# Weights in long contiguous runs, queries and MLP as rows, a TensorE loop of two tiles, and the output in four column strips

## The chip, the cores and the metric

The kernel runs on one core of one Trainium2 chip. The metric is device time in microseconds (us) of that core, over several executions; lower is better. The time of a run is about 1.8 us longer than the span of its trace (1298.81 against 1297.0 for the profiled run of the kernel before); windows and instructions are on the scale of the span.

Some words: a *run* of a load is a stretch of bytes that lies together in memory (elsewhere a run is one execution of a kernel). A load is *issued* when its queue sends it off and *landed* when its data may be used. PSUM is the memory that TensorE writes; copying from there is called evacuation. A line of a TensorE listing gives start and duration in us, the engine, the line of the kernel, output<-inputs, shapes and the number of instructions; in brackets stands how long the engine had waited just before, and for whom.

## The reference, cut to what matters

```python
x  = A_x                                   # 8 sequences, 1 token, D = 640, bf16
xn = layernorm(x)
# attention with a cache: 32 heads, 4096 keys, head size 128
q      = xn @ wq                           # 640 x 4096
scores = q . k_cache * 128**-0.5           # k_cache, v_cache: 8 x 32 x 4096 x 128
o      = softmax(scores) . v_cache
a      = o @ wo                            # 4096 x 640
# channel MLP on the same xn, F = 1728
y = layernorm(xn)
m = gelu(y @ w1 + b1) @ w2 + b2            # 640 x 1728, 1728 x 640
return x + a + m
```

The two caches are 537 MB; wq and wo are 5.2 MB each, w1 and w2 2.2 MB each. All of it is read once, 552 MB in all, so the kernel is a long stream of DMA with work hung beside it.

## The kernel before

One tile t is four heads of one sequence: 4.19 MB of K and 4.19 MB of V, each 128 partitions of 32 KB. There are 64 tiles, and two buffers each for K and V. A quarter of the scores is made on TensorE (transposes of K on TensorE, then products), three quarters on VectorE. Two tiles form a group with one softmax. V is multiplied on TensorE ("PV").

The program is a list of operations. Each has a position; each engine executes its own operations in order of position, and so does the SP queue, which issues nearly all DMAs. What an operation reads (R) and writes (W) sets its semaphores. So an issue that waits in the SP queue holds up every later issue.

```python
add(eng, pos, fn, R=[...], W=[...])        # operation on engine eng, in order of pos
ld(pos, dst, src, W, sem, R=())            # the same for a DMA issued on SP

# weights of the queries in two loads; first four heads first
ld(-99.0, wqa_sb, A_wq[:, 0:QP * P].rearrange("(c k) n -> k c n", k=P), ["wqA"], "wqa")
ld(-93.0, wqb_sb, A_wq[:, QP * P:H * P].rearrange("(c k) n -> k c n", k=P), ["wqB"], "wqb")
# K of tile t at t - 1.5 (tiles 0 and 1: -100 and -94), V of tile t at t + 0.6;
# V0 and V1 lie where the weights lay: they wait for "wqBfree", "wqAfree", "ovfree"
ld(-95.2, w1_sb, B_w1.rearrange("(c k) f -> k c f", k=P), ["ovw1"], "w1")
ld(-95.1, w2_sb[:, 0:FC - 1, :], B_w2[0:(FC - 1) * P, :].rearrange("(c k) n -> k c n", k=P), ["ovw2a"], "w2a")
ld(-95.0, w2_sb[0:FLAST, FC - 1, :], B_w2[(FC - 1) * P:F, :], ["ovw2b"], "w2b")
for hg in range(NG):                       # 8 loads of wo, one for four heads
    ld(hg * B + 2.55, wo_sb[:, :, :], ..., ["wo"], "wo")
# ... (cut: layernorm, scores, softmax, values)
# end: base = x + b2 + MLP + attention of all but the last four tiles, put into PSUM by a product
# with the identity; the last projection is added on top
def pe_last(e):
    for a in range(HT):
        for k in range(2):
            r = e.matmul(TRF[0:B, k, 0:D // 2], oTn_sb[:, a, :],
                         wo_sb[:, a, k * D // 2:(k + 1) * D // 2], start=False, ...)
```

With "(c k) n -> k c n" a partition gets rows k, k+128, k+256 and so on: each row is a run of its own (1 KB for wqa, 7 KB for wqb, 3.4 KB for w1, 1,280 bytes for w2).

## Time and profile before

| quantity | value | view |
|---|---|---|
| time | 1297.73 us (1297.53 to 1297.98, 3 runs) | times |
| bytes moved | 552.04 MB | page, DMA packets |
| steady rate | 8.39 MB in 19.42 us, 432 GB/s | chain of waits, two V landings |
| VectorE, TensorE, ScalarE busy | 86%, 51%, 38% | page |
| end of the DMA stream, end of the span | about 1288.4, 1297.0 | windows of 4 us, span |

The first view is the kernel's page: the span in 40 slices of 32.4 us, with the share of the DMA engines' time (in tenths) and the rate of each slice, and the chain of waits by engine.

```profile
DMA  9999999999999999999999999999999999999997
GB/s 383 399 425 433 431 429 434 426 434 432 428 435 425 436 434 428 432 425 436 434 431 431 425 435 435 431 429 431 429 435 431 429 431 429 436 430 426 433 430 302
...
DMA 86%; PE 9%; DVE 2%; SPq 2%; issue 1%; ACT 0%; DVEq 0%
```

The DMA engines are busy everywhere. The rate is 425 to 436 GB/s from the third slice to the last but one. Only the first two slices and the last are lower, so only there can a change that moves the same bytes gain anything. What is lost in the beginning is seen in windows of 4 us. The columns are busy time of each engine, the granted TensorE clock, the DMA share and GB/s.

```profile
12.00:16.00 4.00, 0.28 (x11) 0.31 (x12) 0.00 (x0) 0.00 (x0) 0.00 (x0) 1.00 0.90 293
32.00:36.00 4.00, 0.00 (x0) 0.00 (x0) 3.96 (x2) 0.00 (x0) 0.00 (x0) 0.50 0.87 367
56.00:60.00 4.00, 3.59 (x57) 3.05 (x55) 0.00 (x0) 2.52 (x4) 0.00 (x0) 0.50 0.80 262
```

The SP queue in the beginning (start, duration, what was issued):

```profile
2.21 17.41 SPq L370 DMA_DIRECT2D w_sb<-in_B_w_dram  x2
...
30.97 0.34 SPq L370 DMA_DIRECT2D KV_sb<-in_A_k_cache_dram  x1
56.29 0.34 SPq L370 DMA_DIRECT2D KV_sb<-in_A_v_cache_dram  x1
```

The two issues of w2 (1,728 runs of 1,280 bytes) hold the queue for 17.4 us. V0 is issued at 56.29 only, when all queries are made and the place of wq is free; K2 alone was in the queue then. That is the dip at 56 to 60. The last 17 us on TensorE:

```profile
1280.06 2.30 PE L745 MATMUL TR_ps<-base_sb,ident_f 8*8 8x320 f32 x4 [0.97 <-DVE base_sb L739]
...
1286.70 1.03 PE L595 MATMUL C_ps<-rs_sb,mask_f 128*128 128x2 f32 x8
1287.66 1.49 PE L619 MATMUL PV_ps<-KV_sb,P_sb 128*16 128x512 bf16 x24
...
1290.99 0.65 PE L629 MATMUL PV_ps<-KV_sb,P_sb 128*4 128x128 bf16 x32 [0.88 <-DMA KV_sb<-in_A_v_cache_dram]
...
1292.51 2.15 PE L669 MATMUL TR_ps<-wo_sb,oTn_sb 128*8 128x320 bf16 x8 [0.26 <-DVE oTn_sb L661]
```

The window in which the stream ends, with the clock (the third number from the right):

```profile
1288.00:1292.00 4.00, 2.06 (x60) 0.84 (x48) 0.00 (x0) 0.86 (x2) 0.00 (x0) 1.00 0.10 41
```

The clock is at its full rate here: rowsum (L595) takes 1.03 us. The 41 GB/s are 0.4 us of a stream at 432, so the stream ends near 1288.4. The base product (L745) ends at 1282.36. Of tile 62's and 63's values, the last 32 PV matmuls wait 0.88 us for the last piece of V. The last projection takes 2.15 us.

### The profile page before, as it was taken

The numbers are of one execution on the slowest core, as the hardware profiler recorded it, in microseconds if no ns is written. First come the engines' busy times: TensorE is split into PE (matmuls) and PEld (weight loads), VectorE is DVE, ScalarE is ACT, GpSimd is POOL, SyncE is SP. The second block draws the span as 40 slices with busy tenths as digits, with TensorE's granted clock in tenths as the row PEclk, the third lists the DMA queues.
The fourth block names the chain that finished last, engine by engine and source line by source line (L and its number), as shares of the span: only waits on it lengthen the run. The fifth ranks groups of instructions, "written<-read, shape, count | busy, mean of one in ns | idle before, by whom it ended". The sixth has DMA issues, their size and how long they took to land.

```text
span 1297.0 us, 19542 instructions
## 1 busy us (share of the span) xinstructions
PE 657.6 (51%) x7884; PEld 428.4 (33%) x7884; DVE 1119.4 (86%) x574; ACT 493.1 (38%) x1202; POOL 0.2 (0%) x4
## 2 busy tenths in 40 slices
PE   4354554555454455444555445544545544545555
PEld 3233333333233243232333233332332332333332
DVE  7698898898898898888988888988988988988884
ACT  2244344334344244343344343343442443432442
POOL 0000000000000000000000000000000000000000
PEclk9555565555555555555555655556655565555556
DMA  9999999999999999999999999999999999999997
GB/s 383 399 425 433 431 429 434 426 434 432 428 435 425 436 434 428 432 425 436 434 431 431 425 435 435 431 429 431 429 435 431 429 431 429 436 430 426 433 430 302
DMA packets 26738, 552.04 MB, mean 426 GB/s; under 512 B 2313, under 2 KB 8801, under 8 KB 10082
## 3 DMA queue, kind: packets, MB, share of 16 engines
q1 hardware_dynamic: 26688, 551.80, 99.4%
q8 instruction: 10, 0.16, 0.1%
q10 hardware_dynamic: 34, 0.02, 0.0%
q14 instruction: 6, 0.05, 0.0%
HBM read 551.80 MB, written 0.01 MB: 425 GB/s over the span
## 4 chain that ended last, share of the span: by engine, by line
DMA 86%; PE 9%; DVE 2%; SPq 2%; issue 1%; ACT 0%; DVEq 0%
DMA KV_sb<-in_A_v_cache_dram 84%; PE PV_ps L619 8%; DMA KV_sb<-in_A_wq_dram 2%; SPq L370 2%; DVE Y_sb L544 1%; DVE Y_sb L548 0%; PE C_ps L457 0%; PE TR_ps L512 0%; ACT KT_sb L515 0%; PE TR_ps L669 0%; ACT qT_sb L462 0%; ACT S_sb L532 0%; PE PV_ps L629 0%; PE S_ps L522 0%; DVE out_sb L749 0%
## 5 line engine op out<-in xcount | busy, mean ns | idle before, releaser
L544 DVE TENSOR_TENSOR Y_sb<-KV_sb,qbc_sb 128x6144 bf16<-128x6144 bf16 x128 | 429.1, 3352 | 93.9 <-DMA KV_sb<-in_A_k_cache_dram 93.9
L551 DVE TENSOR_REDUCE S_sb<-Y_sb 128x48 f32<-128x3072 bf16 x128 | 429.1, 3353 | 4.4
L515 ACT ACTIVATE KT_sb<-TR_ps 128x1024 bf16<-128x1024 bf16 x256 | 254.8, 1021 | 249.2 <-PE TR_ps L512 247.6
L512 PE MATMUL TR_ps<-ident_bf,KV_sb 128*128 128x128 bf16 x2048 | 249.6, 309 | 102.7 <-DMA KV_sb<-in_A_k_cache_dram 84.2
L619 PE MATMUL PV_ps<-KV_sb,P_sb 128*16 128x512 bf16 x2040 | 224.6, 619 | 130.4 <-DMA KV_sb<-in_A_v_cache_dram 130.4
L512 PEld LDWEIGHTS TR_ps<-ident_bf,KV_sb 128*128 128x128 bf16 x2048 | 201.2, 142 | 115.5 <-DMA KV_sb<-in_A_k_cache_dram 89.2
L548 DVE TENSOR_TENSOR Y_sb<-Y_sb 128x3072 bf16<-128x3072 bf16 x128 | 224.9, 1757 | 4.4
L522 PE MATMUL S_ps<-qk_sb,KT_sb 128*128 128x4 bf16 x2048 | 97.9, 170 | 147.4 <-ACT KT_sb L515 145.8
L638 ACT ACTIVATE E_sb<-PV_ps 128x512 bf16<-128x512 f32 (+1 forms) x65 | 38.5, 592 | 319.8 <-PE PV_ps L619 317.9
L522 PEld LDWEIGHTS S_ps<-qk_sb,KT_sb 128*128 128x128 bf16 x2048 | 86.1, 109 | 178.2 <-ACT KT_sb L515 178.2
L619 PEld LDWEIGHTS PV_ps<-KV_sb,P_sb 128*16 128x16 bf16 x2040 | 63.1, 124 | 242.9 <-DMA KV_sb<-in_A_v_cache_dram 136.0
L583 ACT ACTIVATE P_sb<-S_sb,NB_sb 32x128 bf16<-32x128 f32 x256 | 101.9, 398 | 3.8
L644 PE MATMUL C_ps<-sel_bf,E_sb 128*128 128x4 bf16 x256 | 16.9, 172 | 102.6 <-DVE rinv_sb L600 79.3
L565 PE MATMUL CH_ps<-ident_f,M_sb 128*2 128x128 f32 (+1 forms) x33 | 12.2, 370 | 103.7 <-DVE M_sb L563 103.7
L577 ACT ACTIVATE NB_sb<-CH_ps 128x2 f32<-128x2 f32 (+1 forms) x33 | 5.7, 172 | 152.0 <-PE CH_ps L573 152.0
L532 ACT ACTIVATE S_sb<-S_ps 32x32 f32<-32x32 f32 x256 | 48.2, 188 | 31.5 <-PE S_ps L522 29.2
L644 PEld LDWEIGHTS C_ps<-sel_bf,E_sb 128*128 128x128 bf16 x256 | 11.4, 104 | 134.1 <-DVE rinv_sb L600 79.7
L595 PEld LDWEIGHTS C_ps<-rs_sb,mask_f 128*128 128x128 f32 x256 | 42.7, 252 | 24.1 <-issue 24.1
L583 ACT ACTIVATION_READ_ACCUMULATOR P_sb<-S_sb,NB_sb 32x1 f32 x256 | 47.0, 184 | 0.0
L595 PE MATMUL C_ps<-rs_sb,mask_f 128*128 128x2 f32 x256 | 45.4, 299 | 0.0
L565 PEld LDWEIGHTS CH_ps<-ident_f,M_sb 128*2 128x2 f32 (+1 forms) x33 | 2.6, 80 | 106.6 <-DVE M_sb L563 106.6
L661 DVE TENSOR_TENSOR oTn_sb<-C_ps,rinv_sb 128x8 bf16<-128x8 f32 x32 | 4.7, 147 | 26.8 <-issue 22.5
(82 smaller groups left out, 158.6 us busy)
## 6 DMA issues: line engine op xcount, KB each, us to landing
KV_sb<-in_A_k_cache_dram SPq DMA_DIRECT2D x64, 4096.0 KB, 26.8
KV_sb<-in_A_v_cache_dram SPq DMA_DIRECT2D x63, 4096.0 KB, 35.2
wo_sb<-in_A_wo_dram SPq DMA_DIRECT2D x8, 640.0 KB, 28.0
KV_sb<-in_A_wq_dram SPq DMA_DIRECT2D x1, 4480.0 KB, 28.5
KV_sb<-in_B_w_dram SPq DMA_DIRECT2D x1, 2160.0 KB, 19.2
w_sb<-in_B_w_dram SPq DMA_DIRECT2D x1, 2080.0 KB, 24.3
KV_sb<-in_A_v_cache_dram SPq DMA_DIRECT2D x1, 2048.0 KB, 12.7
KV_sb<-in_A_v_cache_dram SPq DMA_DIRECT2D x2, 1024.0 KB, 15.0
```

The lines of the kernel that those rows point to most:

```text
L512: r = e.transpose(TR_ps[:, it.box[0], jj * P:(jj + 1) * P], kv[:, n * BK + jj, :], ident_bf[:, :])
L515: add("act", t - 0.59 + 0.12 * n, lambda e: e.activation(KT_sb[:, m % NS, :, :].rearrange("p a b -> p (a b)"), TR_ps[:, it.box[0], :], ACT ...
L522: r = e.matmul(S_ps[:, c:c + HT], KT_sb[:, m % NS, jj, :], qk_sb[:, :, b % HB], start=True, stop=True)
L532: r = e.activation(S_sb[s, g % SR, i, 0:JP], S_ps[s, 0:JP * HT].rearrange("p (j a) -> p j a", a=HT)[:, :, a], ACT.Copy)
L544: return e.tensor_tensor(y, kv[:, j0:j1, :], qbc_sb[:, g % 2, i, :][:, None, :].to_broadcast([P, nj, P]), ALU.mult)
L548: lambda e, y=y, y2=y2: e.tensor_tensor(y2, y[:, :, 0:P // 2], y[:, :, P // 2:P], ALU.add),
L551: lambda e, y2=y2, j0=j0, j1=j1: e.tensor_reduce(S_sb[:, g % SR, i, j0:j1], y2, AX.X, ALU.add),
L583: r = e.activation(P_sb[s, g % PR, i, :, a, :], S_sb[s, g % SR, i, :].rearrange("p (m c) -> p m c", c=4), ACT.Exp, bias=NB_sb[s, g % 2, i: ...
L595: r = e.matmul(RS_ps[:, a * GT:(a + 1) * GT], mask_f[:, a, :], rs_sb[:, g % PR, :], start=True, stop=True)
L619: r = e.matmul(PV_ps[32 * ct:32 * ct + HT * 4, t % 2, :], P_sb[:, g % PR, i, m, :, :].rearrange("p a c -> p (a c)"), vv[:, 4 * m:4 * m + 4 ...
L638: add("act", pos, lambda e: e.activation(E_sb[:, k, 0:n], PV_ps[:, k, 0:n], ACT.Copy), R=[("PV", k)], W=[("E", k)], X=[("PVb", k)])
L644: r = e.matmul(OT_i, E_sb[:, t % 2, c * P:(c + 1) * P], sel_bf[:, c:HT * 4:4], start=(c == 0), stop=(c == 3 and not last))
```

## The change

Its intent: load the weights in runs of 17 to 40 KB, so that the stream starts at full rate and the SP queue is not held; make queries and the MLP's hidden layer as rows (8 partitions, many columns, few weight loads), so that wq is done sooner and V0 can be issued sooner; make the TensorE loop two tiles long, with a projection after each pair; split the last projection into four column strips that TensorE can work on side by side. Two more edits are cut from the diff below: the probabilities of the softmax have one buffer instead of two, and the evacuation of every second tile's values waits for wo. The diff cut to its core:

```diff
-    FC = (F + P - 1) // P
+    FP, FB = 96, 4                        # 1728 = 96 x 18
+    FC, FW = F // FP, F // FB
-        w2_sb = sb("w2_sb", [P, FC, D], BF)
+        w2_sb = sb("w2_sb", [FP, FC, D], BF)
-        ld(-99.0, wqa_sb, ...); ld(-93.0, wqb_sb, ...)
+        ld(-100.0, wq_sb, A_wq.rearrange("(k c) n -> k c n", c=DC), ["wq"], "wq")
-            pos = (-100.0, -94.0)[t] if t < NK else t - 1.5         # K
+            pos = (-99.0, -94.0)[t] if t < NK else t - 1.5
-            pos = t + 0.6                                            # V
-            R = (["wqBfree"], ["wqBfree", "wqAfree", "ovfree"])[t] if t < NV else []
+            pos = (0.45, 0.55)[t] if t < NV else t + 0.6
+            R = (["wqfree"], ["wqfree", "w1free", "hfree"])[t] if t < NV else []
-        ld(-95.1, w2_sb[:, 0:FC - 1, :], ...); ld(-95.0, w2_sb[0:FLAST, FC - 1, :], ...)
+        ld(-95.1, w2_sb[:, :, :], B_w2.rearrange("(k c) n -> k c n", c=FC), ["w2"], "w2")
-            ld(hg * B + 2.55, wo_sb[:, :, :], ...
+            ld(hg * B + 3.35, wo_sb[:, :, :], ...
... (queries: 8 blocks of 5 matmuls 8 x 512 instead of 160 of 128 x 8; then 32 transposes)
-            elif (g + 1) * GT % HB == 0: ... add("pe", np_ + 0.57, pe_o, ...)
+        for g in range(-1, NGRP - 2):      # a projection for each pair of tiles; oTn zeroed in between
+            add("pe", g * GT + 5.33, pe_o, R=["wo", "oTn"], W=["ACC"], ...)
... (MLP as rows: hidden layer 4 x 432 columns, 18 transposes, second product into the PV banks)
+        add("dve", 0.2, lambda e: e.tensor_tensor(xb2_sb..., PV_ps[0:B, :, 0:D // 2], xb2_sb..., ALU.add),
+            R=["mlp", "xb2"], W=["xb2"], ...)
-                        for k in range(2): r = e.matmul(TRF[0:B, k, 0:D // 2], ...)
+                        for k in range(4): r = e.matmul(TRF[32 * k:32 * k + B, 0, 0:D // 4], ...)
-        add("sp", END + 3, lambda e: e.dma_start(out2[:, :], out_sb[:, :]), ...)
+        for k in range(4): add("sp" if k < 2 else "act", END + 3, ... out2[:, k * D // 4:(k + 1) * D // 4] ...)
-            sch.emit_rolled("pe", e, sems, 2.013, HB)
+            sch.emit_rolled("pe", e, sems, 2.27, GT)
```

## The prediction

> **What bounds the kernel.** The DMA engines. The 40-slice strip shows DMA share 9 in every slice but the last, and 425 to 436 GB/s from slice 3 to 39; the page gives 552.04 MB. The chain of waits is 83.8% "V cache landing". In the steady part a K and a V tile (8.39 MB) take 19.42 us (landings at 169.24 and 208.10 are two tiles apart): 432 GB/s. The Trainium skill ("DMA: Bandwidth & Descriptors", Where 436 GB/s comes from) puts the port ceiling at 435 GB/s; this trace agrees within 1%. VectorE is busy 86%, TensorE 51%; each K load is issued about 17 us before the queue would run dry. The change moves the same bytes, so only stretches where the queue runs below 432 GB/s, and the tail after the last landing, can give time.
>
> **Where time is lost now.** Windows of 4 us: 0-4 at 216 GB/s (first bytes, 2.0 us lost, stays), 12-16 at 293 (1.3 us; wq heads 0-3 come in 1 KB runs), 20-24 at 392 and 32-36 at 367 (0.9 together; w2 comes in 1,280-byte runs), 56-60 at 262 (1.6 us). The last is a gap: V0 may be issued only at 56.29, after wq landed at 48.8 and seven blocks of queries ran, while only K2 was queued. Against 431 GB/s, slices 1 to 3 (383, 399, 425) lack 32.4 x (48+32+6)/431 = 6.5 us, so some 4.5 can come back. Tail: last V piece 1290.95, end 1297.0; in it the projection L669 is 8 matmuls of 320 columns, 2.17 us, and the evacuations 0.48.
>
> **What the change does.**
> 1. wq whole, first in the queue, one 40 KB run per partition; w1 17 KB, w2 23 KB. The two w2 issues that held the SP queue 8.4 and 9.0 us shrink under 1 us.
> 2. Estimates from these rates: wq lands near 15 us, K0 25, w1 30, w2 35, K1 45. Queries are 40 matmuls of 512 columns, at most 0.43 us each (L619 at half clock: four side by side take 0.43), so done at 24 to 32; then V0 is issued, with over 10 us still queued. The gap at 56-60 goes. K2 is issued about 38 to 46, V1 45, K3 56 to 63: the queue stays fed.
> 3. MLP as rows: off the path.
> 4. Loop of two tiles, a projection after every pair (about 0.7 us more each), one buffer for probabilities: TensorE has the slack; steady period stays 19.42.
> 5. Tail: 16 matmuls of 160 columns in four strips. If strips overlap as in L619, 2.17 becomes about 0.6; one evacuation of 160 columns about 0.3 instead of 0.48; four output DMAs, two issues per queue, add 0.4. Net 1.4 us.
>
> Risk: w2 on 96 partitions may load the memory ports unevenly, up to 1.7 us back (estimate: a third of its 5.1 us).
>
> **Prediction.** 1297.7 - 4.3 - 1.4 = 1292.0 us (0.4% faster), range 1289.5 to 1295.0. Faster by over 2%: 0.01; within 2%: 0.985; slower: 0.005.
>
> **What would show it.** Slices 1 and 2 above 410 and 425 GB/s; no 4 us window below 380 between 4 and 100 us; SP weight issues under 1 us; V landings still two tiles per 38.85 us; last landing near 1286.5; last projection near 0.6 us; end 4.6 us after the last landing.
>
> **What would make it wrong.** The queue drains because V0 or K2 comes late; a new wait in the steady loop (projection before the wo load, single probability buffer) exceeding 17 us of slack; strips that do not overlap; small output writes that complete later.

## The result, and the profile after

The changed kernel takes 1303.14 us (1301.45 to 1304.34, 4 runs); the kernel before took 1297.86 beside it (1297.53 to 1301.29, 4 runs). The ratio is 1.0034, with a 95% interval of 1.0012 to 1.0055. A ratio here is the mean time of one kernel's runs over that of the other's of the same rounds, so it is not quite the ratio of the medians. With more rounds (e11 below) the ratio is 1.0018 (1.0004 to 1.0033). So the change costs 0.2 to 0.3%, where a gain of 0.4% was predicted.

The page of the changed kernel, the same lines:

```profile
DMA  9998999999999999999999999999999999999996
GB/s 385 378 434 379 435 434 428 429 434 429 430 434 434 425 433 435 433 424 435 432 431 428 434 429 429 434 435 424 434 435 432 431 430 432 431 429 431 432 427 292
...
DMA 57%; DVE 29%; issue 8%; PE 4%; SPq 0%; ACT 0%; DVEq 0%
```

The second and the fourth slice have fallen to 378 and 379 GB/s. The chain has moved to K and vector work, but this says little: the chain only follows one path, and the DMA share shows that the stream still fills the steady part. Two K landings of the chain (164.04 and 202.89 with the wait after them) are 38.85 us apart as before, so the steady period is unchanged.

The windows that are new:

```profile
28.00:32.00 4.00, 2.29 (x57) 1.88 (x56) 0.85 (x1) 2.39 (x6) 0.00 (x0) 1.00 1.13 334
32.00:36.00 4.00, 2.91 (x48) 2.57 (x48) 3.96 (x2) 3.53 (x5) 0.00 (x0) 0.56 1.09 242
36.00:40.00 4.00, 4.00 (x18) 1.12 (x15) 3.96 (x3) 1.53 (x2) 0.00 (x0) 0.58 1.00 243
108.00:112.00 4.00, 3.01 (x45) 2.43 (x45) 2.47 (x5) 2.42 (x10) 0.00 (x0) 0.50 0.16 47
```

There are two losses. From 28 to 40 us the DMA engines are fully busy (share 1.09, 1.09, 1.00) and yet move only 334, 242 and 243 GB/s. Against 432 that is (98 + 190 + 189) x 4 / 432 = 4.4 us. By the order of the queue w2 is being loaded then. From 108 to 112 the share is 0.16: the queue is empty for (432 - 47) x 4 / 432 = 3.6 us. The SP queue shows who let it run empty:

```profile
2.14 0.86 SPq L372 DMA_DIRECT2D w_sb<-in_B_w_dram  x1
...
28.07 0.33 SPq L372 DMA_DIRECT2D KV_sb<-in_A_v_cache_dram  x1
...
67.61 18.69 SPq L372 DMA_DIRECT2D KV_sb<-in_A_k_cache_dram  x2
...
110.25 0.39 SPq L372 DMA_DIRECT2D wo_sb<-in_A_wo_dram  x1
110.82 0.36 SPq L372 DMA_DIRECT2D KV_sb<-in_A_k_cache_dram  x1
```

w2 is issued in 0.86 us, as was hoped, and V0 at 28.07. But the first load of wo goes out at 110.25 only, and K5 (110.82) stands behind it. And VectorE has a new wait: the addition of the MLP's result waits 6.9 us for the second product.

```profile
DVE xb_sb L740 <- PE PV_ps L736: 6.9, 1, 6.9
```

The last 17 us on TensorE:

```profile
1286.66 0.72 PE L767 MATMUL TR_ps<-xb_sb,ident_f 8*8 8x160 f32 x8 [0.97 <-DVE xb_sb L761]
...
1291.73 1.84 PE L600 MATMUL C_ps<-rs_sb,mask_f 128*128 128x2 f32 x8
1293.51 2.74 PE L624 MATMUL PV_ps<-KV_sb,P_sb 128*16 128x512 bf16 x24
...
1297.15 1.05 PE L634 MATMUL PV_ps<-KV_sb,P_sb 128*4 128x128 bf16 x32
...
1299.09 0.70 PE L673 MATMUL TR_ps<-wo_sb,oTn_sb 128*8 128x160 bf16 x16 [0.26 <-DVE oTn_sb L665]
```

The strips work: the last projection takes 0.70 us, the base product 0.72. But nothing in these lines waits for DMA any more. From 1286.66 to the last 32 PV matmuls TensorE pauses only for ScalarE's evacuations (twice, 0.7 us), at half clock. Rowsum takes 1.84 us where it took 1.03 before, and the next 24 PV matmuls 2.74 where they took 1.49. The window in which the stream ends (near 1292.4):

```profile
1292.00:1296.00 4.00, 4.00 (x32) 2.19 (x31) 0.21 (x1) 0.00 (x0) 0.00 (x0) 0.50 0.11 45
```

So the two profiled runs differ in the clock at their ends too. e11 below profiles the changed kernel with the high clock.

### The profile page after: what moved, and what is told of

Same layout as the page of the kernel before. It is cut to its first block, busy times and chain, and to the rows that moved or that the text cites. A ratio compares the mean times of both kernels' runs of the same rounds, so it can differ in the third digit from the quotient of the medians.

```text
span 1302.6 us, 20062 instructions
## 1 busy us (share of the span) xinstructions
PE 680.7 (52%) x8046; PEld 440.0 (34%) x8046; DVE 1123.5 (86%) x592; ACT 499.5 (38%) x1237; POOL 0.2 (0%) x4
## 4 chain that ended last, share of the span: by engine, by line
DMA 57%; DVE 29%; issue 8%; PE 4%; SPq 0%; ACT 0%; DVEq 0%
DMA KV_sb<-in_A_k_cache_dram 56%; DVE Y_sb L549 18%; DVE Y_sb L553 6%; DVE S_sb L556 4%; DMA KV_sb<-in_A_wq_dram 1%; PE TR_ps L457 1%; PE PV_ps L736 1%; PE PV_ps L624 0%; PE TR_ps L712 0%; PE ACC_ps L684 0%; SPq L372 0%; DVE M_sb L568 0%; PE CH_ps L570 0%; PE TR_ps L725 0%; DVE M_sb L572 0%
```

## The experiments

Eleven runs were made: nine new kernels (e1 to e9), e7 once more (e10) and the changed kernel once more (e11). All gave correct results. "Before" in each call was 1297 to 1303 us, with medians of 1300.0, 1300.0 and 1299.5. Single runs of every kernel scatter by 2 to 5 us. One cause of that comes out in e4 and e7, and it limits what medians of a few runs can say. Windows and issue times are sharper.

### e1: w2 on 128 partitions

```diff
-        ld(-95.1, w2_sb[:, :, :], B_w2.rearrange("(k c) n -> k c n", c=FC), ["w2"], "w2")
+        ld(-95.1, w2_sb[:, 0:C2, :], B_w2[0:FM, :].rearrange("(k c) n -> k c n", c=C2), ["w2"], "w2")  # 13 rows each
+        ld(-95.0, w2_sb[0:R2, C2, :], B_w2[FM:F, :], ["w2b"], "w2b")                                   # 64 rows left
   (and the transposes and the second product in 13 chunks of 128 and one of 64)
```

> The changed kernel with w2 on 128 partitions again: 13 rows of 1,280 bytes in one run per partition, and 64 rows left over. Theory A (96 partitions make w2 slow, about 4.4 us of queue time lost between 28 and 40 us): no window of 4 us between 20 and 48 us below 390 GB/s. Theory B (long runs beside compute are slow): still below 300. Since the next issue behind w2 that stalls the queue, the wo load at 110 us, hangs on vector and TensorE work and not on w2, theory A further expects the gap before wo to grow from 3.6 to 5-6 us and the time to fall by only about 2 us (the second product has 28 matmuls instead of 36), to 1301. If the two losses were independent, it would fall by 4.4, to 1298.7.

Measured: 1297.89 us (1297.11 to 1299.26, 4 runs), ratio to before 0.9982 (0.9964 to 1.0000). The windows:

```profile
28.00:32.00 4.00, 3.29 (x51) 2.92 (x51) 2.79 (x1) 2.96 (x7) 0.00 (x0) 0.63 0.99 426
32.00:36.00 4.00, 3.24 (x34) 1.82 (x33) 3.93 (x3) 3.56 (x4) 0.00 (x0) 0.94 1.03 396
36.00:40.00 4.00, 3.39 (x18) 1.06 (x17) 4.00 (x2) 1.58 (x4) 0.00 (x0) 1.00 1.07 456
104.00:108.00 4.00, 2.64 (x45) 2.35 (x44) 2.89 (x4) 3.17 (x14) 0.00 (x0) 0.50 0.28 81
```

The loss from 28 to 40 us is all but gone, with runs of 16.6 KB, so theory A stands against B. The gap before wo stays (81 GB/s, and 328 in the window before it: 4.2 us together). That it would eat up most of the gain was wrong: with w2 quicker, K1 and the tiles after it land sooner, wo went out at 105.47 instead of 110.25, and the two losses added up as if independent.

### e2: the MLP addition later

```diff
-        add("dve", 0.2, lambda e: e.tensor_tensor(xb2_sb..., PV_ps..., ...
+        add("dve", 1.14, lambda e: e.tensor_tensor(xb2_sb..., PV_ps..., ...
-        add("pe", 0.3, pe_zero, ...
+        add("pe", 1.95, pe_zero, ...
```

> The changed kernel with the addition of the MLP result moved behind the vector work of tile 1, and the zeroing of PV behind it. Theory: this addition waits 6.9 us for the second MLP product with K1 landed behind it, which delays K3 and everything after by 7 us, so that the queue runs dry at 108 us. Then DVE starts tile 1 near 48.5 instead of 55.8, K3 is issued near 61, wo near 103, no window near 108 below 380 GB/s, time 3 to 4 us lower, about 1299.5. Rival (the gap comes only from the place of wo in the queue behind the projection): gap stays about 3.6 us, time unchanged.

Measured: 1301.64 us (1301.0 to 1303.48, 4 runs), ratio to before 1.0011 (0.9993 to 1.0030). The theory fell: K3 was issued at 63.32 instead of 67.61, but wo still at 109.77, and the gap stayed (67 GB/s from 108 to 112, 3.4 us). The 6.9 us that VectorE waits for the MLP are not what empties the queue. They end in an earlier wait for K2 instead.

### e3: wo behind K and V

```diff
-            ld(hg * B + 3.35, wo_sb[:, :, :],
+            ld(hg * B + 3.65, wo_sb[:, :, :],
```

> The changed kernel with each wo load moved behind the next K and V load in the SP queue. Theory: the first wo load waits for TensorE's first projection at 110.2 and holds K5, which could be issued at 102.7 when vector work on K3 is done; so the gap of 3.6 us before 111 goes and the time falls by 3 to 4 us, to 1299.5. Rival (vector work too late for any order): gap stays. No effect on steady windows in either.

Measured: 1299.35 us (1297.88 to 1301.58, 4 runs), ratio to before 0.9995 (0.9972 to 1.0018). The SP queue:

```profile
102.77 0.33 SPq L372 DMA_DIRECT2D KV_sb<-in_A_k_cache_dram  x1
...
110.13 0.39 SPq L372 DMA_DIRECT2D wo_sb<-in_A_wo_dram  x1
```

wo is issued at the same time as in the changed kernel (110.13 against 110.25), but K5 goes out at 102.77, and the window from 108 to 112 moves 426 GB/s. The gap was made by the place of the wo load in the queue. Its wait is for TensorE's projection L684, which stands behind the softmax of tiles 2 and 3 in the order of TensorE. By the code this first projection (`g = -1`) works on zeros: wo and oTn have only been set to zero by then. So the first load of wo waits for a product that adds nothing; leaving that product out was not tried.

### e4 and e7: all three edits, and two of them

e4 has the edits of e1, e2 and e3; e7 those of e1 and e3.

> All three edits together. Theory: w2 loss (4.4) and gap (3.6) both gone, so 8 us less than the changed kernel, 1295, and 2.5 us less than the kernel before. Windows between 4 and 120 us all above 380 GB/s. If there is a third loss I have not seen, it stays above 1296.5.

> w2 on 128 partitions and wo behind K and V, without the later MLP addition. Theory (the order of wo alone makes the gap; the vector wait for the MLP is made up while K2 is awaited): the same as with all three, 1293.3, no window below 380 between 8 and 120 us. Rival (the MLP wait costs by itself): 1 us or more above that.

Measured: e4 1293.34 us (1293.12 to 1296.12, 4 runs), ratio to before 0.9949 (0.9931 to 0.9967); e7 1295.55 (1293.49 to 1296.22, 4 runs), ratio 0.9969 (0.9951 to 0.9987). In both, all windows from 16 to 120 us are above 390 GB/s (that from 12 to 16 is at 383 in e4 and 375 in e7, a little under the 380 that e7's expectation set), and the stream ends alike (57 and 51 GB/s in the window from 1284 to 1288, so some 0.5 us after 1284). The intervals of the two ratios overlap. The edit of e2 brings nothing that these runs resolve.

The lowest time of each is within 0.4 us of the other's, and both have runs near 1296. The profiled runs show why. They ended with different clocks: e4 (span 1294.3) with the low one, e7 (span 1291.7) with the high one. TensorE in e4, then in e7:

```profile
1279.10 3.59 PE L627 MATMUL PV_ps<-KV_sb,P_sb 128*16 128x512 bf16 x32
...
1283.52 1.84 PE L603 MATMUL C_ps<-rs_sb,mask_f 128*128 128x2 f32 x8
1285.29 2.74 PE L627 MATMUL PV_ps<-KV_sb,P_sb 128*16 128x512 bf16 x24
...
1288.93 1.05 PE L637 MATMUL PV_ps<-KV_sb,P_sb 128*4 128x128 bf16 x32
...
1290.86 0.70 PE L676 MATMUL TR_ps<-wo_sb,oTn_sb 128*8 128x160 bf16 x16 [0.26 <-DVE oTn_sb L668]
```

```profile
1283.61 1.03 PE L603 MATMUL C_ps<-rs_sb,mask_f 128*128 128x2 f32 x8
1284.57 1.47 PE L627 MATMUL PV_ps<-KV_sb,P_sb 128*16 128x512 bf16 x24
...
1286.93 0.65 PE L637 MATMUL PV_ps<-KV_sb,P_sb 128*4 128x128 bf16 x32
...
1288.45 0.45 PE L676 MATMUL TR_ps<-wo_sb,oTn_sb 128*8 128x160 bf16 x16 [0.26 <-DVE oTn_sb L668]
```

The rowsum starts at 1283.52 and 1283.61. From there on the same instructions take 1.84 against 1.03, 2.74 against 1.47, 1.05 against 0.65 and 0.70 against 0.45 us. The granted clock from 1284 to 1288 is 0.50 in e4 and 1.00 in e7. The difference of the spans, 2.6 us, is this clock and nothing else that the traces show. The Trainium skill ("TensorE: Matmul & The Clock Gate", Part 1) describes a gate with half and full clock, set by recent activity in a free-running window of about 3.4 us, so that the moment of the switch varies from run to run. These traces agree as to the two levels and the variation; that the phase of that window decides which case a run gets is not shown here.

### e5 and e6: is it the 96 partitions?

e5 is the changed kernel with w2 on 96 partitions still, but one row of 1,280 bytes per run. e6 is the kernel before with nothing but w2 on 96 partitions, in runs of 23 KB.

```diff
 e5
-        ... B_w2.rearrange("(k c) n -> k c n", c=FC) ...      h_sb[:, j:F:FC]
+        ... B_w2.rearrange("(c k) n -> k c n", k=FP) ...      h_sb[:, j * FP:(j + 1) * FP]
 e6 (kernel before)
-        ld(-95.1, w2_sb[:, 0:FC - 1, :], ...); ld(-95.0, w2_sb[0:FLAST, FC - 1, :], ...)
+        ld(-95.1, w2_sb[:, :, :], B_w2.rearrange("(k c) n -> k c n", c=FC), ["ovw2a"], "w2a")   # FP = 96, FC = 18
-        ... w1_sb[:, kc, c * P:c * P + rows] ...
+        ... w1_sb[:, kc, c:F:FC] ...          (also b1; base_sb and out_sb share other buffers for space)
```

> The changed kernel with w2 on 96 partitions still, but in runs of 1,280 bytes (one row each) instead of 23 KB. Theory A1 (the 96 partitions are what is slow): windows between 28 and 40 us again near 240 GB/s, time 1302 to 1304. Rival A2 (runs of 23 KB at this pitch are slow, the partition count is not): these windows above 360 GB/s as with 1,280-byte runs in the kernel before, time about 1299.

> The kernel before with w2 alone changed: one run of 23 KB on each of 96 partitions, MLP in columns as it was (with strided weights), two small buffers shared. Theory A1: w2's stretch, some 15 to 30 us in, has windows near 240 GB/s, and the kernel is 3 to 4 us slower than the kernel before, about 1301 where that is 1297.7. Rival (w2 is only slow behind the wq of the changed kernel or beside its rows of MLP): no such window, time as before or 0.9 us better.

Measured: e5 1303.81 us (1301.8 to 1305.0, 4 runs), ratio to before 1.0026 (1.0005 to 1.0046); e6 1303.73 (1301.73 to 1306.39, 4 runs), ratio 1.0037 (1.0016 to 1.0057). The windows of e5, then of e6:

```profile
28.00:32.00 4.00, 3.02 (x45) 2.62 (x44) 2.48 (x1) 3.01 (x6) 0.00 (x0) 0.67 0.98 288
32.00:36.00 4.00, 3.24 (x41) 1.98 (x40) 3.93 (x3) 3.43 (x4) 0.00 (x0) 0.91 1.11 210
```

```profile
20.00:24.00 4.00, 3.22 (x45) 2.61 (x43) 3.95 (x2) 3.53 (x4) 0.00 (x0) 1.00 1.07 251
24.00:28.00 4.00, 3.77 (x26) 3.69 (x26) 3.98 (x2) 1.46 (x2) 0.00 (x0) 1.00 1.07 236
```

Short runs on 96 partitions are as slow as long ones, and in the other kernel, behind other loads and beside other work, 96 partitions are slow again. So the 96 partitions (always 0 to 95; no others were tried) are the cause, and neither the run length nor what is loaded or computed beside them. The rate is about half of 432. The Trainium skill ("SBUF — State Buffer", Door 1: The DMA port swizzle) says that partitions 0 to 63 reach only eight of sixteen memory ports and 64 to 127 the other eight, so that 64 partitions load at half the rate. It has no row for 96. Two estimates from its table and its 27.2 GB/s per port: if all ports worked to the end, the busiest, with eight of the 96 partitions, would need 6.8 us. If each of sixteen engines took six neighbouring partitions in order, which is an assumption, engines would often share a port, and the load would take 8.5 us, where 432 GB/s give 5.1 us. The windows of the changed kernel show 5.1 + 4.4 = 9.5 us. The second estimate is nearer, but no view here shows ports or which engine takes which partition, so the mechanism is argued and not shown.

### e8: what the strips are worth

All three edits of e4, with the last projection, the base product and the output as in the kernel before.

> All three edits, but the last projection in two halves of 320 columns and one output DMA, as before. My prediction's step 5 says the strips are worth 1.4 us in all: then 1294.7. From the traces (projection 2.17 to 0.70, evacuation 0.48 to 0.32, output 1.74 to 2.40) I now expect 0.9 to 1.0: 1294.3. If the base product in strips (2.3 to 0.7 us, on TensorE ahead of the last PV) counts too, 2.5: 1295.8.

Measured: 1297.14 us (1295.37 to 1299.05, 4 runs), ratio to before 0.9975 (0.9953 to 0.9998). Its profiled run has the low clock at the end, as that of e4:

```profile
1278.44 2.30 PE L773 MATMUL TR_ps<-xb_sb,ident_f 8*8 8x320 f32 x4 [0.97 <-DVE xb_sb L767]
...
1285.09 1.84 PE L603 MATMUL C_ps<-rs_sb,mask_f 128*128 128x2 f32 x8
...
1292.44 2.30 PE L676 MATMUL TR_ps<-wo_sb,oTn_sb 128*8 128x320 bf16 x8 [0.26 <-DVE oTn_sb L668]
```

The spans are 1297.1 and 1294.3. The strips save 2.8 us at the low clock: the base product 1.58 (2.30 to 0.72), the last projection 1.60 (2.30 to 0.70), the evacuation 0.16 (0.48 to 0.32), less a longer output. From the issue of the output to the end of the span e8 has 1297.1 - 1295.32 = 1.8 and e4 1294.3 - 1291.97 = 2.3 us. Of the lowest runs of each, e8 is 2.25 us above e4. So at the low clock the strips were worth about twice the 1.4 us of the prediction, which had left out the base product.

### e9, e10 and e11: the end freed from TensorE, and repetitions

e9 is e7 with the projection of tiles 58 and 59 and the base's way to rows moved from behind tile 63's softmax to before tile 62's scores. e10 is e7 again, e11 the changed kernel again.

```diff
-            add("pe", g * GT + 5.33, pe_o, ...
+            add("pe", g * GT + 5.33 if g < NGRP - 3 else 61.39, pe_o, ...
-        add("dve", fp, ... resT_sb ...); add("pe", fp + .02, pe_fin, ...); add("dve", fp + .04, dve_base, ...)
+        add("dve", 61.392, ... resT_sb ...); add("pe", 61.394, pe_fin, ...); add("dve", 61.396, dve_base, ...)
```

> As e7 (w2 on 128 partitions, wo behind K and V), and the last projection of tiles 58 and 59 and the residual's way to rows taken out of the last 4 us before PV of tile 62, to before the scores of tile 62. Theory: in all traces so far PV of tile 62 starts only when the base product ends, 22.3 us after K63's vector work starts, though its V has landed and its probabilities are ready; TensorE then has work without a gap to the end, so its granted clock decides the end (rowsum 1.03 or 1.84 us, 24 PV matmuls 1.47 or 2.74). With PV62 some 3 us earlier the last piece of V is what the end waits for: 1 us faster than e7 where the clock was high (span 1291.7), 3 us where it was low (1294.3), runs closer together, median about 1292.5. Rival (the end hangs on the last landing already): no change.

> e7 again, beside e9 on the same chip, for the difference of the two and for the spread: 1293.3 when TensorE runs at the high clock in the last 10 us, 1296.1 when not; mean near 1294.8.

> The changed kernel again with more rounds: between 1301.4 (high clock at the end) and 1304.4 (low), mean 1303, so 3 to 5 us over the kernel before, whose runs go from 1297.3 to 1301.9.

Measured: e9 1294.33 us (1293.61 to 1295.82, 5 runs), ratio to before 0.9959 (0.9945 to 0.9974); e10 1294.44 (1293.11 to 1298.18, 6 runs), ratio 0.9964 (0.9948 to 0.9981); e11 1301.65 (1301.13 to 1303.66, 5 runs), ratio 1.0018 (1.0004 to 1.0033). TensorE in e9:

```profile
1276.59 3.59 PE L627 MATMUL PV_ps<-KV_sb,P_sb 128*16 128x512 bf16 x32 [0.64 <-DMA KV_sb<-in_A_v_cache_dram]
...
1283.96 0.70 PE L627 MATMUL PV_ps<-KV_sb,P_sb 128*16 128x512 bf16 x8 [0.95 <-DMA KV_sb<-in_A_v_cache_dram]
...
1286.41 1.06 PE L637 MATMUL PV_ps<-KV_sb,P_sb 128*4 128x128 bf16 x32 [0.79 <-DMA KV_sb<-in_A_v_cache_dram]
```

The mechanism came as expected: PV of tile 62 starts at 1276.59 instead of about 1279.1, and the last two groups wait for pieces of V again. The worth did not. The medians of e9 and e10 differ by 0.1 us. Only the worst runs are better (1295.82 against 1298.18). The end is now 5.4 us after the last piece of V is used (1286.41 to 1291.8), and what is left of the scatter is not explained by these runs.

The profiled run of e11 is the changed kernel with the high clock at the end (rowsum 1.03 us, 24 PV matmuls 1.47, last projection 0.45):

```profile
1292.00:1296.00 4.00, 2.74 (x64) 1.47 (x64) 0.29 (x2) 0.87 (x2) 0.00 (x0) 1.00 0.06 25
```

Its stream ends near 1292.2 and its span is 1299.3: a tail of 7.1 us.

## Why the prediction was wrong, point by point

Two terms failed, both in the first 120 us of the stream: step 2, "the queue stays fed" (3.6 us), and the risk of w2 on 96 partitions, feared at up to 1.7 us and left out of the sum (4.4 us).

- **What bounds the kernel, and the steady part: right.** DMA stream, 432 GB/s, steady period 38.85 us for two tiles in both kernels. The longer TensorE loop body and the single buffer for probabilities cost nothing there. The wo loads do wait for the projection (194.5 us in eight waits, in the list of the SP queue's waits), but in the steady part the queue is deep enough.
- **The start (4.3 us): about right in size, once nothing undoes it.** In e7 the stream ends near 1284.5, where it ended near 1288.4 in the kernel before: 3.9 us. Step 1 was right (SP issues under 1 us, no 1 KB runs), and V0 at 28.07 was within the 24 to 32 predicted.
- **The risk of w2 on 96 partitions: mis-sized.** The prediction put it at "up to 1.7 us (a third of its 5.1 us)" and left it out of the sum. It measured 4.4 us: the load ran at about half the rate, not at two thirds. The estimate had counted the bytes per port and had let all ports work in parallel to the end.
- **Step 2, "the queue stays fed": this step failed.** The prediction followed V0, K2, V1 and K3 and stopped there. The first wo load stands ahead of K5 in the SP queue, and waits for a projection behind the softmax of tiles 2 and 3. The 17 us of slack quoted for the steady part do not exist in the first pass: the gap cost 3.6 us. e3 took it away by the order alone. "A new wait (projection before the wo load)" was on the list of what would make the prediction wrong, but the slack was read in the wrong place. K3, predicted at 56 to 63, was issued at 67.61.
- **Step 3, "MLP as rows: off the path": wrong as said, harmless in effect.** VectorE waited 6.9 us for it and K3 was late, but e2 shows that the time gained there is lost again in waiting for K2.
- **Step 5, the tail (1.4 us): mechanism right; what it is worth hangs on the clock.** The strips overlap (0.70 us at half clock, 0.45 at full), and e8 against e4 gives 2.8 us at the low clock. With the high clock the tail is 7.1 us in the changed kernel (e11) and 8.6 in the kernel before: 1.5 us less, near the prediction, though some of it is clock again: the last projection of the kernel before had fallen back to the low clock (2.15 us; 1.25 with the high one in e6). The base stood behind tile 63's softmax before, too; the new order puts a projection (L684, 0.69 us) between them, and TensorE then has work up to the last PV matmuls but for two pauses of 0.7 us. Whether a run gets the high or the low clock there is worth 2.6 us (e4 against e7), or 3.3 in the changed kernel (1302.6 against 1299.3). The prediction had no term for that; which clock a run gets is luck as far as these runs show. "End 4.6 us after the last landing" did not apply: the end no longer hung on the last landing. The wait for the last piece of V is not in every run of the old order either: e6's last PV matmuls do not wait for it.

The sum: the stream of the changed kernel ends near 1292.4, that is 1288.4 - 3.9 + 4.4 + 3.6 = 1292.5. The tail after the end of the stream is 10.2 us at the low clock (1302.6 - 1292.4) and 8.6 in the kernel before's profiled run (1297.0 - 1288.4). Together the spans differ by 5.6 us. But the kernel before had the high clock in that run: against e11 the difference is 2.3 us, 3.8 later in the stream and 1.5 shorter in the tail. The prediction was 5.7 us less, so it missed by 8.0 us there, and the 4.4 of w2 and the 3.6 of the wo load make these up. The other 3.3 us of the run shown above are the clock. With both faults mended (e7, e10) the change is a gain: 0.9964 to 0.9969 of the kernel before, 4 to 5 us, 1294.44 us in the longer set. This is near the 1292.0 that was predicted, but still above it.

What stays open: the port mechanism of the 96 partitions, the reason why a run gets one clock or the other at the end, and the rest of the scatter in e9. The change's larger parts (queries as rows, MLP as rows, the loop of two tiles) were not undone one by one.

## What to carry to other kernels

When a stream is the bound, walk every load in its queue, in order, through the first pass, and ask for each what it waits for and what stands behind it; slack read in the steady part says nothing about the start. A load that waits for compute belongs behind the loads that do not. Change the number of partitions of a DMA only with a measurement of its rate: long runs on 96 partitions were slower than short ones on 128.

## What the Trainium skill lacked or had wrong

- "SBUF — State Buffer", Door 1, has rate rows for 4, 16, 32, 64 and 128 partitions but none between 64 and 128, and "DMA: Bandwidth & Descriptors" (How many engines) names a tile of 96 partitions as one that uses all 16 engines. Here a load on 96 partitions had all engines busy (share 1.0 to 1.1) at 240 GB/s, about half of the 432 of 128 partitions. Sixteen busy engines did not mean the full rate.
- "DMA: Bandwidth & Descriptors" (Where 436 GB/s comes from) says in its warning that for HBM to SBUF the HBM side, about 358 GB/s per core, binds. In this kernel on one core, 1,297 us of such loads went at 426 GB/s on the whole and 432 in the steady part. That is within 1% of the page's 435 for the ports, and the single-core 425 of the same page (Measured) is nearer too: the warning lacks the condition that the other core of the pair streams as well.
- "TensorE: Matmul & The Clock Gate" (Part 1) puts the cost of the clock's ramp at under 1% of a typical span and says not to fit to a specific count of slow matmuls. That holds here, with 0.2% of the span (2.6 us between e4 and e7), but this is as large as the effect under study; in the tail of a DMA-bound kernel it has to be looked at run by run.
